# Routing attention and a gated FFN on one core: query halves outermost, exponentials in PSUM, and a weight rounding over three engines

## The chip, the core and the metric

The kernel runs on one core of one Trainium2 chip. A core has a matrix engine (TensorE, PE in the tables, with PEld for its weight loads), a vector engine (VectorE, DVE), a scalar engine (ScalarE, ACT), GpSimd (POOL) and SyncE (SP), which here issues DMAs. SBUF is the working memory, PSUM the memory into which TensorE writes. Each engine runs its own instructions in order, and engines wait for each other by semaphores. The metric is the device time of one execution in microseconds (us); the kernel before takes 1363.32 us, the median of three runs from 1362.93 to 1364.97.

## The reference

Attention over 4 batches and 8 heads, 768 queries and keys, head size 64. Each query and each key is assigned to one of 16 centroids of its head, and a query attends only to keys of its own cluster. The heads' outputs stand side by side as 512 features of 3072 tokens, and an FFN with 2048 hidden units follows.

```
q_assign = argmax(q_n @ c_n.T); k_assign = argmax(k_n @ c_n.T)     # 16 clusters
mask   = q_assign[:, :, :, None] == k_assign[:, :, None, :]
scores = where(mask, (q @ k.T) / sqrt(64), -1e9)
attn   = softmax(scores);  x = attn @ v                            # (4, 8, 768, 64)
h = x.reshape(3072, 512) @ w_in                                    # w_in (512, 2048), float64
out = (h * sigmoid(1.702 * h)) @ w_out                             # w_out (2048, 512), float64
```

The two weights arrive as 64-bit floats and are rounded to 32 bits on the chip from their high and low words.

## The kernel before, in words

Two heads make a pair, 16 pairs in all, four to a batch. A *unit* is 128 keys against half of the queries (384) of a pair: `scores` (L314) gives two 384-column matrix products into a PSUM tile `s`, `weigh` (L325) takes the exponential on ACT into an SBUF tile `A` (L329) and lets DVE zero, in place, what lies outside the cluster, one instruction for each head (L331), `add_up` (L338) adds the units' `A` on POOL for the denominator (L347), and `values` (L350), two units later, multiplies by V (L357). Six units make a *group* (one half of a pair's queries), twelve a pair, 48 a batch, 192 in all. After a group `normalise` (L364) sums over keys on PE (L372), takes the reciprocal on DVE (L375) and scales (L377, L380).

When all eight groups of a batch are there, `ffn_chunks` puts 56 *chunks* into a queue: for each half of the queries 16 of the first product (`first`, L397, with tanh on ACT at L402 and a multiply on DVE at L405) and 12 of the second (`second`, L416: four products of 512 columns each; four such chunks make one block of the output, which is then written out). The loop over units (L444) takes 1.33 chunks a unit from the queue, so that the FFN of a batch runs between the units of the next one. The last batch's 56 chunks run behind everything else (L483).

Preparing a pair (transposes of Q and K, nearest centroid, the codes spread over all partitions as `qb` by a DMA round trip) is eight steps, `PREP`, one a unit, during the pair before (L462). In the same loop, `round_w` (L145) rounds the weights, 64 pieces of 256 columns, 1.5 a unit: DVE masks the bits of the mantissa and shifts the exponent (L153, L155), POOL scales and clamps (L158 to L162), DVE joins (L164 to L168), POOL multiplies (L170).

The order on each engine is the order of the code (the scheduler is set to manual). PSUM has eight banks: two tiles `s` of two banks, one `o`, and three `m` for everything else.

Of the kernel before, what the change touches and what calls it, by code (L numbers as in the profile page):

```python
# [11 lines left out]
U32 = mybir.dt.uint32  # L12
AF = mybir.ActivationFunctionType
# [24 lines left out]
def fast(  # L38
# [58 lines left out]


    qk_in, v_in = {}, {}

    def load_qk(p):
        for w, src in enumerate((q, k)):
            t = inp.tile([P, NJ, 2, D], FP32, name=f"in{w}")
            b, hp = divmod(p, HP)
            for a in range(2):
                nc.sync.dma_start(
                    out=t[:, :, a, :],
                    in_=src[b, 2 * hp + a].rearrange("(p j) d -> p j d", j=NJ))
            qk_in[p, w] = t

    def load_v(p):
        b, hp = divmod(p, HP)
        t = inp.tile([P, 2, NJ, D], FP32, name="inv", bufs=3)
# [6 lines left out]
    cent = const.tile([P, D], FP32, name="cent")  # L120
    nc.scalar.dma_start(out=cent, in_=centroids.rearrange("h c d -> (h c) d"))
    load_qk(0)
    load_v(0)
    load_qk(1)
    load_v(1)

    w_in = const.tile([P, NCH, DF], FP32, name="w_in")
    w_out = const.tile([P, NF, DM], FP32, name="w_out")
    WN = 256
# [6 lines left out]
    w_raw = {}  # L136

    def load_w(i):
        if i < len(w_chunks):
            t = wp.tile([P, WN, 2], I32, name="raw")  # L140
            nc.sync.dma_start(out=t.rearrange("p n t -> p (n t)"),
                              in_=w_chunks[i][1])
            w_raw[i] = t

    def round_w(i):  # L145


        raw = w_raw.pop(i)
        hi, lo = raw[:, :, 1], raw.bitcast(U32)[:, :, 0]
        m, e, one_m = (hp_pool.tile([P, HALF], FP32, name="g")[:, 0:WN]  # L150
                       for _ in range(3))
        m, e = m.bitcast(I32), e.bitcast(I32)
        nc.vector.tensor_scalar(out=m, in0=hi, scalar1=0xFFFFF, scalar2=None,  # L153
                                op0=ALU.bitwise_and)
        nc.vector.tensor_scalar(out=e, in0=hi, scalar1=20, scalar2=0x7FF,  # L155
                                op0=ALU.logical_shift_right,
                                op1=ALU.bitwise_and)
        nc.gpsimd.tensor_scalar(out=one_m, in0=m, scalar1=2.0 ** -20,  # L158
                                scalar2=1.0, op0=ALU.mult, op1=ALU.add)
        nc.gpsimd.tensor_scalar(out=e, in0=e, scalar1=896 + 255.0,  # L160
                                scalar2=896.0, op0=ALU.min, op1=ALU.max)
        nc.gpsimd.tensor_scalar(out=e, in0=e, scalar1=-896.0, scalar2=1.0,  # L162
                                op0=ALU.add, op1=ALU.mult)
        nc.vector.scalar_tensor_tensor(out=one_m, in0=lo, scalar=2.0 ** -52,  # L164
                                       in1=one_m, op0=ALU.mult, op1=ALU.add)
        nc.vector.tensor_scalar(out=e, in0=e, scalar1=23, scalar2=None,  # L166
                                op0=ALU.logical_shift_left)
        nc.vector.scalar_tensor_tensor(out=e, in0=hi, scalar=-2 ** 31, in1=e,  # L168
                                       op0=ALU.bitwise_and, op1=ALU.bitwise_or)
# [3 lines left out]
    for i in range(3):  # L173
        load_w(i)
# [7 lines left out]
    nc.vector.memset(half, 0.5)  # L182
    ones = const.tile([P, D], FP32, name="ones")
# [9 lines left out]
    csq = const.tile([P, D], FP32, name="csq")  # L193
# [9 lines left out]
    cc = const.tile([P, 2, D], FP32, name="cc")  # L203
# [21 lines left out]
    def prep_turn(p, i):  # L225
        w, h = divmod(i, 2)
        if h == 0:
            T[p, w] = trp.tile([P, S], FP32, name=f"T{w}")
# [7 lines left out]
        if h:  # L236
# [4 lines left out]
    def prep_near(p):  # L241
# [11 lines left out]
        sT[p] = asg.tile([P, HALF], FP32, name="sT")  # L253
        nc.scalar.copy(sT[p], ps[:, 0:HALF])

    def prep_assign(p):
# [9 lines left out]
        eq = asg.tile([P, n, NC], FP32, name="eq")  # L266
# [7 lines left out]
        code[p] = asg.tile([P, NH, 2, 2, 2], FP32, name="code")  # L274
# [8 lines left out]
    def prep_spread(p):  # L283
# [6 lines left out]
        row = asg.tile([n, P], BF16, name="row")  # L290
        nc.vector.tensor_copy(out=row, in_=ps[0:n, 0:P])
        line = dram.tile([n, P], BF16, name="line")
        nc.sync.dma_start(out=line, in_=row)
        qb = trp.tile([P, 2, S], BF16, name="qb")
# [7 lines left out]
    PREP += [prep_near, prep_assign, lambda p: None, prep_spread]  # L302


    UP = 2 * NJ
    NU = NPAIR * UP
    s_of, A_of, sum_of, o_of, O_of, xT_of = {}, {}, {}, {}, {}, {}

    def split(u):
        p, r = divmod(u, UP)  # L310
        h, kt = divmod(r, NJ)
        return p, h, kt

    def scores(u):  # L314
        p, h, kt = split(u)
# [7 lines left out]
        s_of[u] = ps[:, :, 0:HALF]  # L323

    def weigh(u):  # L325

        p, h, kt = split(u)
        A = ap.tile([P, 2, HALF], FP32, name="A")
        nc.scalar.activation(out=A, in_=s_of.pop(u), func=AF.Exp, scale=SCALE)  # L329
        for a in range(2):  # L330
# [4 lines left out]
                in1=A[:, a, :], op0=ALU.is_equal, op1=ALU.mult)  # L335
        A_of[u] = A

    def add_up(u):  # L338
        if u % NJ == 0:
            return  # L340
        g = u // NJ
        if u % NJ == 1:
            sum_of[g] = ap.tile([P, 2, HALF], FP32, name="sum", bufs=2)
            first = A_of[u - 1]
        else:
            first = sum_of[g]
        nc.gpsimd.tensor_tensor(out=sum_of[g], in0=first, in1=A_of[u],  # L347
                                op=ALU.add)

    def values(u):  # L350
        p, h, kt = split(u)
        g = u // NJ
# [7 lines left out]
        if kt == NJ - 1:  # L360
            O_of[g] = op.tile([P, HALF], FP32, name="O")
            nc.scalar.copy(O_of[g], o_of.pop(g)[:, 0:HALF])

    def normalise(g):  # L364

        p, h = divmod(g, 2)
        if h == 0:
            xT_of[p] = xp.tile([P, S], FP32, name="xT", bufs=2 * NCH)
# [5 lines left out]
        rec = op.tile([P, HALF], FP32, name="rec")  # L374
        nc.vector.reciprocal(out=rec, in_=ps[:, 0:HALF])  # L375
        O = O_of.pop(g)
        nc.vector.tensor_tensor(out=xT_of[p][:, h * HALF:(h + 1) * HALF],  # L377
                                in0=O, in1=rec, op=ALU.mult)

        nc.vector.scalar_tensor_tensor(  # L380
            out=O, in0=ps[:, 0:HALF], scalar=1.0, in1=rec, op0=ALU.mult,
            op1=ALU.max, accum_out=sums[:, g:g + 1])
        if g % (2 * HP) == 2 * HP - 1:
            ffn.extend(ffn_chunks(p // HP))
# [4 lines left out]
    def ffn_chunks(b):  # L389
        xT = [xT_of.pop(b * HP + c) for c in range(NCH)]  # L390
        hs, ys = {}, {}

        def first(h, f):

            ps = bank()
            for c in range(NCH):
                nc.tensor.matmul(out=ps[:, 0:HALF],  # L397
                                 lhsT=w_in[:, c, f * P:(f + 1) * P],
                                 rhs=xT[c][:, h * HALF:(h + 1) * HALF],
# [37 lines left out]
    for step in PREP:  # L437
        step(0)
# [487 lines left out]
```

## Time and profile before

| what | us |
|---|---|
| median of three runs | 1363.32 |
| the profiled execution | 1362.06 |
| its span, first to last instruction | 1360.3 |
| PE busy | 1170.5 (86%) |
| DVE busy | 618.4 (45%) |
| POOL busy | 446.5 (33%) |
| ACT busy | 271.8 (20%) |
| TensorE's mean granted clock | 0.916 of 2.4 GHz |

The page of the profile gives the busy share of each engine in 40 slices of the span, the granted clock of TensorE beside it, and the groups of instructions by line. A share of the whole span says little here, since the program has stages of different kinds: units with rounding and no FFN, units with FFN, and FFN alone. Each is to be read by itself.

### The profile page before, as it was taken

How to read it: one execution, taken by the hardware profiler on the slowest of the kernel's cores; microseconds unless marked ns; L12 is line 12 of the kernel's file. 1: busy time of each engine (PE TensorE's matmuls, PEld its weight loads, DVE VectorE, ACT ScalarE, POOL GpSimd, SP SyncE). 2: the span in 40 equal slices, each digit the busy share in tenths (PEclk: the TensorE clock that was granted, in tenths of full speed). 3: DMA queues.
4: the chain of work that ended last, by engine and by line, in shares of the span. 5: the costliest groups of instructions: out<-in, count | busy, mean ns of one | idle time of the engine just before them, and what ended most of it. 6: DMA issues, size and time to landing. Idle time of an engine off the chain costs nothing. (4 is left out here: it accounts for less than half of the span.)

```text
span 1360.3 us, 10636 instructions
## 1 busy us (share of the span) xinstructions
PE 1170.5 (86%) x3842; PEld 490.1 (36%) x3842; DVE 618.4 (45%) x1104; ACT 271.8 (20%) x425; POOL 446.5 (33%) x424
## 2 busy tenths in 40 slices
PE   6555455454699999999999999999999999799997
PEld 2111111111244344433443444334434443354553
DVE  4656666667864335434642354356423542320110
ACT  2111111111233113212231132132312321110110
POOL 3666666666632222223322222233222222200000
PEclk8667667677799999999999999999999999899999
DMA  6122222221210010102100101021000000000000
GB/s 163 47 66 82 66 66 70 64 71 59 46 35 13 19 51 1 40 15 62 36 12 20 51 4 44 8 62 35 12 20 16 11 2 16 9 0 14 10 1 25
DMA packets 70095, 49.11 MB, mean 36 GB/s; under 512 B 52624, under 2 KB 56720, under 8 KB 70032
## 3 DMA queue, kind: packets, MB, share of 16 engines
q1 hardware_dynamic: 69888, 48.30, 12.6%
q8 instruction: 32, 0.52, 0.1%
q14 instruction: 31, 0.25, 0.1%
q10 hardware_dynamic: 144, 0.03, 0.0%
HBM read 41.98 MB, written 6.34 MB: 36 GB/s over the span
## 5 line engine op out<-in xcount | busy, mean ns | idle before, releaser
L347 POOL TENSOR_TENSOR sum<-sum,A 128x768 f32<-128x768 f32 x128 | 233.7, 1826 | 437.5 <-DVE A L331 437.5
L331 DVE SCALAR_TENSOR_TENSOR A<-qb,code,A 128x384 f32<-128x384 bf16 x384 | 259.5, 718 | 247.3 <-ACT A L329 242.4
L357 PE MATMUL o<-A,inv 128*64 128x384 f32 x768 | 228.8, 569 | 158.7 <-DVE A L331 139.1
L397 PE MATMUL m<-xT,w_in 128*128 128x384 f32 x1024 | 353.9, 497 | 1.5 <-DVE bad L480 1.1
L416 PE MATMUL m<-w_out,g 128*128 128x512 f32 x768 | 345.3, 600 | 0.0
L329 ACT ACTIVATE A<-s 128x768 f32<-128x768 f32 x192 | 155.6, 810 | 529.7 <-PE s L319 497.6
L397 PEld LDWEIGHTS m<-xT,w_in 128*128 128x128 f32 x1024 | 189.8, 191 | 160.5 <-issue 26.9
L416 PEld LDWEIGHTS m<-w_out,g 128*128 128x128 f32 x768 | 141.6, 190 | 185.4 <-issue 182.6
L319 PE MATMUL s<-T,T 64*128 64x384 f32 x768 | 194.0, 585 | 0.0
L405 DVE SCALAR_TENSOR_TENSOR g<-th,m 128x384 f32<-128x384 f32 x128 | 70.8, 553 | 223.1 <-ACT th L402 222.8
L357 PEld LDWEIGHTS o<-A,inv 128*64 128x64 f32 x768 | 52.8, 147 | 319.5 <-DVE A L331 190.6
L347 POOL TENSOR_TENSOR sum<-A 128x768 f32<-128x768 f32 x32 | 59.5, 1860 | 196.4 <-DVE A L331 194.2
L402 ACT ACTIVATE th<-m 128x384 f32<-128x384 f32 x128 | 62.7, 490 | 264.4 <-PE m L397 260.6
L375 DVE RECIPROCAL rec<-m 128x384 f32<-128x384 f32 x32 | 81.7, 2553 | 34.6 <-PE m L372 34.6
L319 PEld LDWEIGHTS s<-T,T 64*128 64x128 f32 x768 | 63.8, 204 | 87.0 <-issue 72.3
L164 DVE SCALAR_TENSOR_TENSOR g<-raw,g 128x256 f32<-128x256 uint32 x64 | 27.2, 425 | 62.8 <-POOL g L158 62.8
L160 POOL TENSOR_SCALAR g<-g 128x256 int32<-128x256 int32 x64 | 40.8, 638 | 5.1
L166 DVE TENSOR_SCALAR g<-g 128x256 int32<-128x256 int32 x64 | 18.8, 294 | 49.8 <-POOL g L162 49.8
L422 ACT ACTIVATE y<-m 128x512 f32<-128x512 f32 x24 | 14.3, 597 | 128.6 <-PE m L416 115.5
L231 PE MATMUL m<-ident,in 128*128 128x128 f32 x192 | 39.4, 323 | 0.3 <-DMA in<-in_k_dram 0.2
L170 POOL TENSOR_TENSOR w_out<-g 128x256 f32<-128x256 f32 x32 | 29.9, 933 | 27.9 <-DVE g L168 27.9
L170 POOL TENSOR_TENSOR w_in<-g 128x256 f32<-128x256 f32 x32 | 29.5, 923 | 27.9 <-DVE g L168 27.9
(54 smaller groups left out, 381.7 us busy)
## 6 DMA issues: line engine op xcount, KB each, us to landing
raw<-in_moe_w_in_dram SPq DMA_DIRECT2D x32, 256.0 KB, 2.7
raw<-in_moe_w_out_dram SPq DMA_DIRECT2D x32, 256.0 KB, 2.6
in<-in_q_dram SPq DMA_DIRECT2D x32, 192.0 KB, 4.1
in<-in_k_dram SPq DMA_DIRECT2D x32, 192.0 KB, 4.3
inv<-in_v_dram SPq DMA_DIRECT2D x16, 384.0 KB, 3.2
qb<-line SPq DMA_DIRECT2D x16, 384.0 KB, 3.5
out_dram<-y SPq DMA_DIRECT2D x24, 256.0 KB, 2.0
line<-row SPq DMA_DIRECT2D x16, 3.0 KB
```

What stands on the lines that cost most here:

```text
L160: nc.gpsimd.tensor_scalar(out=e, in0=e, scalar1=896 + 255.0, scalar2=896.0, op0=ALU.min, op1=ALU.max)
L170: nc.gpsimd.tensor_tensor(out=w_chunks[i][0], in0=one_m, in1=e.bitcast(FP32), op=ALU.mult)
L319: nc.tensor.matmul(out=ps[:, a, 0:HALF], lhsT=T[p, 1][rows, kt * P:(kt + 1) * P], rhs=T[p, 0][rows, h * HALF:(h + 1) * HALF], start=True, ...
L329: nc.scalar.activation(out=A, in_=s_of.pop(u), func=AF.Exp, scale=SCALE)
L331: nc.vector.scalar_tensor_tensor(out=A[:, a, :], in0=qcode[p][:, a, h * HALF:(h + 1) * HALF], scalar=code[p][:, kt % NH, 1, kt // NH, a:a ...
L347: nc.gpsimd.tensor_tensor(out=sum_of[g], in0=first, in1=A_of[u], op=ALU.add)
L357: nc.tensor.matmul(out=o_of[g][a * D:(a + 1) * D, 0:HALF], lhsT=v_in[p][:, a, kt, :], rhs=A[:, a, :], start=(kt == 0), stop=(kt == NJ - 1))
L375: nc.vector.reciprocal(out=rec, in_=ps[:, 0:HALF])
L397: nc.tensor.matmul(out=ps[:, 0:HALF], lhsT=w_in[:, c, f * P:(f + 1) * P], rhs=xT[c][:, h * HALF:(h + 1) * HALF], start=(c == 0), stop=(c = ...
L402: nc.scalar.activation(out=th, in_=ps[:, 0:HALF], func=AF.Tanh, scale=0.851)
L405: nc.vector.scalar_tensor_tensor(out=g, in0=th, scalar=1.0, in1=ps[:, 0:HALF], op0=ALU.add, op1=ALU.mult)
L416: nc.tensor.matmul(out=ps[:, 0:DM], lhsT=hs[h, f][:, n * P:(n + 1) * P], rhs=w_out[:, f, :], start=(f == 0), stop=(f == NF - 1))
```

## The change

A pair's two query halves are no longer done one behind the other. Within a batch all four pairs are done for the first half, then all four for the second, and after four groups the FFN of that half (28 chunks) enters the queue. The loop turns once for two units (*turn t*, 96 in all, three to a group, 12 to a half): two units' scores and exponentials, half of the turn's FFN chunks, preparation steps, rounding, two units' masks and sums, two units' values of the turn before, a normalisation where one is due, and the other FFN chunks. The chunk rate is 28 in 11.5 turns.

The exponential is written back over the scores in PSUM, and the mask reads it there and writes `A` in SBUF. The codes `qb` are 8-bit. The weights are rounded in 32 pieces of 512 columns: DVE cuts the exponent and the mantissa out (`split_w`), ACT scales both, DVE joins the piece before (`join_w`), and POOL does the one multiply. Two thirds of a piece a turn are rounded in the first 12 turns, 2.3 a turn after that. Two pairs are prepared ahead of the loop, pairs 2 and 3 in turns 0 to 5, later ones 20 to 1 turns or so ahead at one step a turn.

```diff
-    def round_w(i):
-        raw = w_raw.pop(i)
...
-        nc.gpsimd.tensor_tensor(out=w_chunks[i][0], in0=one_m,
-                                in1=e.bitcast(FP32), op=ALU.mult)
+    def split_w(i):
+        hi = w_raw[i][:, :, 1]
+        w = w_chunks[i][0]
+        e = wp.tile([P, WN], I32, name="e", bufs=2)
+        nc.vector.tensor_scalar(out=e, in0=hi, scalar1=EXP, scalar2=None,
+                                op0=ALU.bitwise_and)
+        nc.vector.tensor_scalar(out=w.bitcast(I32), in0=hi, scalar1=0xFFFFF,
+                                scalar2=None, op0=ALU.bitwise_and)
+        nc.scalar.activation(out=e, in_=e, func=AF.Relu, scale=8.0,
+                             bias=low[:, 0:1])
+        nc.scalar.activation(out=w, in_=w.bitcast(I32), func=AF.Copy,
+                             scale=2.0 ** -20, bias=1.0)
+    def join_w(i):
+        raw, e, w = w_raw.pop(i), w_pow.pop(i), w_chunks[i][0]
+        nc.vector.scalar_tensor_tensor(
+            out=e, in0=raw[:, :, 1], scalar=-2 ** 31, in1=e,
+            op0=ALU.bitwise_and, op1=ALU.bitwise_or)
+        nc.vector.scalar_tensor_tensor(
+            out=w, in0=raw.bitcast(U32)[:, :, 0], scalar=2.0 ** -52, in1=w,
+            op0=ALU.mult, op1=ALU.add)
+        nc.gpsimd.tensor_tensor(out=w, in0=w, in1=e.bitcast(FP32),
+                                op=ALU.mult)
+    def round_to(n):
+        while w_done[0] <= min(n, NW):
+            i = w_done[0]
+            if i < NW:
+                load_w(i + 2)
+                split_w(i)
+            if i:
+                join_w(i - 1)
+            w_done[0] += 1
...
+        s = s_of[u] = ps[:, :, 0:HALF]
+        nc.scalar.activation(out=s, in_=s, func=AF.Exp, scale=SCALE)
...
-        nc.scalar.activation(out=A, in_=s_of.pop(u), func=AF.Exp, scale=SCALE)
...
-                in1=A[:, a, :], op0=ALU.is_equal, op1=ALU.mult)
+                in1=s[:, a, :], op0=ALU.is_equal, op1=ALU.mult)
...
-    for u in range(NU + DEN):
...
+    for t in range(NT + 2):
+        us = range(2 * t, 2 * t + 2) if t < NT else ()
+        for u in us:
+            scores(u)
+        owed = owed + rate if ffn else 0.0
+        n = min(int(owed), len(ffn))
+        owed -= n
+        for _ in range((n + 1) // 2):
+            ffn.popleft()()
+        for p, i in prep_at.get(t, ()):
+            prep(p, i)
+        round_to(int(t * 2 / 3 if t < TB / 2 else
+                     TB / 3 + (t - TB / 2) * 2.3) - 1)
+        for u in us:
+            mask(u)
+        if 1 <= t <= NT:
+            for u in range(2 * t - 2, 2 * t):
+                values(u)
+        if t >= 2 and (t - 2) % TG == TG - 1:
+            normalise((t - 2) // TG)
+        for _ in range(n // 2):
+            ffn.popleft()()
```

On PE, where the first FFN chunks stand (`s` scores, `o` values, `m<-x,w_in` or `m<-xT,w_in` an FFN chunk of four products), the kernel before has one unit at a time:

```order
L319 MATMUL s<-T_1547,T_1624 128x384 x2
L397 MATMUL m<-xT,w_in 128x384 x4
L357 MATMUL o<-A,inv 64x384 x2
L259 MATMUL m<-ident,sT 128x128 x3
L319 MATMUL s<-T_1547,T_1624 128x384 x2
L397 MATMUL m<-xT,w_in 128x384 x4
L357 MATMUL o<-A,inv 64x384 x2
L319 MATMUL s<-T_1547,T_1624 128x384 x2
L397 MATMUL m<-xT,w_in 128x384 x8
L357 MATMUL o<-A,inv 64x384 x2
```

On PE in the changed kernel, turns 14 to 16, the first with FFN:

```order
L344 MATMUL s<-T_151,T_165 128x384 x4
L417 MATMUL m<-x,w_in 128x384 x4
L379 MATMUL o<-A,inv 64x384 x4
L417 MATMUL m<-x,w_in 128x384 x4
L344 MATMUL s<-T_209,T_223 128x384 x4
L417 MATMUL m<-x,w_in 128x384 x4
L379 MATMUL o<-A,inv 64x384 x4
L417 MATMUL m<-x,w_in 128x384 x4
L344 MATMUL s<-T_209,T_223 128x384 x4
L417 MATMUL m<-x,w_in 128x384 x8
```

The scores of two units now stand together, and so do the values of two units; FFN chunks stand between them on both sides. The two score tiles of a turn are both of the two that exist.

On DVE, the rounding ahead of a unit's masks (L331) in the stage without FFN, in the kernel before, with two pieces:

```order
L153 TENSOR_SCALAR g<-raw 128x256
L155 TENSOR_SCALAR g<-raw 128x256
L164 SCALAR_TENSOR_TENSOR g<-raw,g 128x256
L166 TENSOR_SCALAR g<-g 128x256
L168 SCALAR_TENSOR_TENSOR g<-raw,g 128x256
L153 TENSOR_SCALAR g<-raw 128x256
L155 TENSOR_SCALAR g<-raw 128x256
L164 SCALAR_TENSOR_TENSOR g<-raw,g 128x256
L166 TENSOR_SCALAR g<-g 128x256
L168 SCALAR_TENSOR_TENSOR g<-raw,g 128x256
L331 SCALAR_TENSOR_TENSOR A<-qb,code,A 128x384 x2
```

On DVE in the changed kernel, turn 15: the FFN multiplies (L424, one of turn 14 and one of turn 15), two pieces split and joined, and the masks of two units (L358, four instructions):

```order
L424 SCALAR_TENSOR_TENSOR g<-g,m 128x384 x2
L158 TENSOR_SCALAR e<-raw 128x512
L160 TENSOR_SCALAR w_in<-raw 128x512
L170 SCALAR_TENSOR_TENSOR e<-raw,e 128x512
L173 SCALAR_TENSOR_TENSOR w_in<-raw,w_in 128x512
L158 TENSOR_SCALAR e<-raw 128x512
L160 TENSOR_SCALAR w_in<-raw 128x512
L170 SCALAR_TENSOR_TENSOR e<-raw,e 128x512
L173 SCALAR_TENSOR_TENSOR w_in<-raw,w_in 128x512
L358 SCALAR_TENSOR_TENSOR A<-qb,code,s 128x384 x4
```

A piece's joining (L170, L173) now stands behind the splitting of the next piece, so it reads what ACT made earlier. The masks of the turn stand behind all of it, and behind the multiply of the turn's first FFN chunk.

## Rows read from the trace of the kernel before

**Rows 1.** the stages by windows: engines' busy us (instructions), granted clock, DMA share, GB/s

```profile
13.60:374.90 361.30, 194.64 (x554) 59.80 (x553) 240.44 (x486) 52.56 (x74) 230.96 (x298) 0.70 0.23 67
374.90:1173.60 798.70, 798.24 (x2802) 339.49 (x2800) 349.08 (x558) 195.96 (x307) 211.62 (x118) 1.00 0.09 25
1173.60:1184.60 11.00, 4.19 (x20) 1.21 (x18) 5.61 (x10) 1.29 (x2) 2.61 (x2) 0.78 0.06 22
1184.60:1352.50 167.90, 167.84 (x448) 86.37 (x448) 17.73 (x32) 18.66 (x37) 0.00 (x0) 0.98 0.02 9
```

**Rows 2.** timeline, stage without FFN: start, length, engine, line, [idle before <-releaser]

```profile
184.98 0.43 DVE L164 SCALAR_TENSOR_TENSOR g<-raw,g 128x256 f32<-128x256 uint32 x1 [0.37 <-POOL g L158]
...
186.19 0.29 DVE L166 TENSOR_SCALAR g<-g 128x256 int32<-128x256 int32 x1 [0.78 <-POOL g L162]
...
187.52 2.54 PE L357 MATMUL o<-A,inv 128*64 128x384 f32 x4 [7.41 <-DVE A L331]
```

**Rows 3.** timeline of PE where FFN sets in, same columns

```profile
363.95 2.07 PE L357 MATMUL o<-A,inv 128*64 128x384 f32 x4 [1.89 <-DVE A L331]
...
366.79 1.18 PE L319 MATMUL s<-T,T 64*128 64x384 f32 x4
...
374.05 0.92 PE L319 MATMUL s<-T,T 64*128 64x384 f32 x4
374.90 2.85 PE L397 MATMUL m<-xT,w_in 128*128 128x384 f32 x8
377.67 0.87 PE L357 MATMUL o<-A,inv 128*64 128x384 f32 x4
...
389.76 5.43 PE L397 MATMUL m<-xT,w_in 128*128 128x384 f32 x16
```

**Rows 4.** timeline of the start: first work, masks, rounding, POOL beside them

```profile
5.00 1.51 PE L231 MATMUL m<-ident,in 128*128 128x128 f32 x6
...
13.66 1.65 PE L319 MATMUL s<-T,T 64*128 64x384 f32 x4
...
18.87 1.15 DVE L331 SCALAR_TENSOR_TENSOR A<-qb,code,A 128x384 f32<-128x384 bf16 x2 [4.88 <-DMA qb<-line]
...
26.17 0.72 POOL L170 TENSOR_TENSOR w_in<-g 128x256 f32<-128x256 f32 x1 [0.87 <-DVE g L168]
26.21 0.84 DVE L155 TENSOR_SCALAR g<-raw 128x256 int32<-128x256 int32 x1
...
29.29 1.61 DVE L331 SCALAR_TENSOR_TENSOR A<-qb,code,A 128x384 f32<-128x384 bf16 x2
...
31.05 1.80 POOL L347 TENSOR_TENSOR sum<-sum,A 128x768 f32<-128x768 f32 x1 [0.56 <-DVE A L331]
31.29 1.71 DVE L153 TENSOR_SCALAR g<-raw 128x256 int32<-128x256 int32 x1
```

**Rows 5.** groups by line: busy, mean ns | idle before, releaser

```profile
L375 DVE RECIPROCAL rec<-m 128x384 f32<-128x384 f32 x32 | 81.7, 2553 | 34.6 <-PE m L372 34.6
L405 DVE SCALAR_TENSOR_TENSOR g<-th,m 128x384 f32<-128x384 f32 x128 | 70.8, 553 | 223.1 <-ACT th L402 222.8
...
L402 ACT ACTIVATE th<-m 128x384 f32<-128x384 f32 x128 | 62.7, 490 | 264.4 <-PE m L397 260.6 <-DVE A L331 3.8
...
L164 DVE SCALAR_TENSOR_TENSOR g<-raw,g 128x256 f32<-128x256 uint32 x64 | 27.2, 425 | 62.8 <-POOL g L158 62.8
...
L166 DVE TENSOR_SCALAR g<-g 128x256 int32<-128x256 int32 x64 | 18.8, 294 | 49.8 <-POOL g L162 49.8
...
L471 DVE TENSOR_SCALAR ok<-sums 128x32 f32<-128x32 f32 x1 | 0.2, 180 | 0.0
```

**Rows 6.** the same, from 374.9 to 1173.6

```profile
L397 PE MATMUL m<-xT,w_in 128*128 128x384 f32 x768 | 268.3, 496 | 0.5 <-DVE O L380 0.3
L416 PE MATMUL m<-w_out,g 128*128 128x512 f32 x576 | 262.6, 602 | 0.0
```

**Rows 7.** timeline of PE at the end of the attention

```profile
1173.62 1.51 PE L357 MATMUL o<-A,inv 128*64 128x384 f32 x8
```

More of the change, by code (lines that the diff above doesn't have):

```diff
@@ L12 @@
 U32 = mybir.dt.uint32
+U8 = mybir.dt.uint8
 AF = mybir.ActivationFunctionType
@@ L227, in prep_turn @@
         if h == 0:
-            T[p, w] = trp.tile([P, S], FP32, name=f"T{w}")
+            T[p, w] = pairs.tile([P, S], FP32, name=f"T{w}")
         ps = bank()
@@ L424, in second @@
                     out=out[b * S:(b + 1) * S, :].rearrange(
-                        "(p j) n -> p j n", j=NJ)[:, j, :], in_=y)
-        chunks = []
-        for h in range(2):
-            chunks += [lambda h=h, f=f: first(h, f) for f in range(NF)]
-            chunks += [lambda j=j, part=part: second(j, part)
-                       for j in range(h * NH, (h + 1) * NH)
-                       for part in range(NF // 4)]
-        return chunks
-    for step in PREP:
-        step(0)
-    LAG = 2
@@ L440, in fast @@
-    DEN = 4
-    rate = (2 * NF + NJ * (NF // 4)) / (HP * UP - 6)
-    owed = 0.0
-    w_next = 0
-    for u in range(NU + DEN):
-        p, r = divmod(u, UP)
-        if u < NU:
-            scores(u)
-            if r == 0 and p + 2 < NPAIR:
-                load_qk(p + 2)
-            if r == 3 and p + 2 < NPAIR:
-                load_v(p + 2)
-            weigh(u)
-            add_up(u)
+                        "(p j) n -> p j n", j=NJ)[:, h * NH + n, :], in_=y)
+        return ([lambda f=f: first(f) for f in range(NF)]
+                + [lambda n=n, part=part: second(n, part)
+                   for n in range(NH) for part in range(NF // 4)])
@@ new lines, in fast @@
+    NT = NU // 2
+    TG = NJ // 2
+    TB = 2 * HP * TG
+    prep_at = {}
+    for p in range(2, NPAIR):
+        b, hp = divmod(p, HP)
+        for i, step in enumerate(PREP):
+            if b == 0:
+                t = (hp - 2) * TG + i * TG // len(PREP)
+            else:
+                t = b * TB + (-20, -8, -2, 1)[hp] + i
+            prep_at.setdefault(t, []).append((p, i))
+    loads = deque((p, w) for p in range(NPAIR) for w in range(2))
+    for _ in range(3):
+        loads.popleft()
@@ L454, in fast, with prep @@
+    def prep(p, i):
+        if i == 0 and p:
+            load_v(p)
+        PREP[i](p)
+        if i in (1, 3) and loads:
+            load_qk(*loads.popleft())
+    rate = (NF + NH * (NF // 4)) / (TB / 2 - 0.5)
+    owed = 0.0
+    for p in range(2):
+        for i in range(len(PREP)):
+            prep(p, i)
+    for t in range(NT + 2):
+        us = range(2 * t, 2 * t + 2) if t < NT else ()
+        for u in us:
+            scores(u)
         owed = owed + rate if ffn else 0.0
-        while owed >= 1.0 and ffn:
+        n = min(int(owed), len(ffn))
+        owed -= n
+        for _ in range((n + 1) // 2):
```

201 lines of the change are left out of this document (87 added, 114 removed).

## The prediction

> **What bounds the kernel now.** I read the profile in stages, first by windows, since the page's slices show two kinds of stretch: PE half busy at a granted clock near 0.7, then PE full at 1.00. The rows by stage [rows 1] are to be seen as five prices. From 13.6 to 374.9 us 52 units run without any FFN, 6.95 us each; PE is busy 195 of 361 us, at a clock that switches between the two levels of 1.2 and 2.4 GHz, DVE 240 and POOL 231. From 374.9 to 1173.6 the other 140 units run with 168 FFN chunks, PE is busy all the time at 2.4 GHz, and DVE 349 of 799 us. Then come 11 us for the last group and the check, 167.9 us of FFN alone (56 chunks, 3.0 us each), and from 1352.5 the last write, 7.8 us to the span's end.
>
> The timeline of the first stage says why it is slow [rows 2]: within one rounding piece DVE waits for POOL (0.37 us ahead of L164, 0.78 ahead of L166), since the two pass it back and forth, the masks of the unit stand behind it on DVE, and PE's values wait 7.41 us for the masks. Where rounding has ended and FFN has not set in [rows 3], three units take 374.05 - 366.79 = 7.26 us, 2.42 each, with a preparation and a normalisation among them. So the first stage is bound by DVE and POOL taking turns at the weights, the second by PE, and the fourth by PE.
>
> **The change, part by part.** The sum is over the same five stages, from the start on.
>
> *Start.* Two pairs are prepared ahead of the first unit, where there was one. The first pair takes from 5.00 to 13.66 us [rows 4]; the second repeats these 8.7 us on the same chain of engines. First unit: 22 us (18 if half of it fits into the waits of the first, 28 if K of pair 1, now behind two 512 KB weight loads on SP's queue, comes late).
>
> *Units without FFN.* These are now the 14 turns before a half batch is normalised, 28 units instead of 52. Per turn: two units at 2.42 us, 4.84; ahead of its masks two thirds of a rounding piece. Price of a piece of 512 columns: the plain mask instruction is 180 ns at 32 columns and 294 at 256 [rows 5], so about 0.42 us at 512; the two-tensor one 425 ns at 256 and 553 at 384, so about 0.69. Two of each make 2.2 us, and the ping-pong with POOL goes, since a piece is joined a step after ACT has scaled it. POOL keeps one multiply: 0.72 us at 256 columns, 1.80 for a sum of 768 [rows 4], so about 1.26. Two thirds of 2.2, with some blocking by POOL, is 1.8 us a turn. The codes of pairs 2 and 3 are spread in the turn in which they are found, so PE waits twice for DVE; I put 0.4 a turn for it. 4.84 + 1.8 + 0.4 = 7.0, times 14 = 98 us. Ends: 68 (the rounding hides beside PE) and 126 (9 a turn, PE at 1.2 GHz: scores 1.65 and values 2.54 us [rows 4, 2], twice, and a little).
>
> *Units with FFN.* 164 units (28 to 191) and seven halves, 196 chunks: 112 of the first product and 84 of the second. Prices from this stage alone [rows 6]: 268.3 / 96 = 2.79 us for a first chunk, 262.6 / 72 = 3.65 for a second one, and what is left of 798.7, 267.8 / 140 = 1.91, for a unit with its share of preparation and normalising. 313 + 306 + 314 = 933 us. Two units' values in a row take 1.51 us where one takes 0.87 [rows 7, 3], 0.23 saved in a turn; if scores in a row do the same, 82 turns save 38, if neither carries over, none. I take the middle, 19: 914 us.
>
> *What is late next.* Score tiles are now held until the masks have read them, and there are two, both used in a turn. So a turn is at least: two scores, the FFN chunks of its first part, tanh, multiply, rounding, the first unit's masks; then PE may write scores again. Without rounding that is 1.7 + 2.79 + 0.49 + 0.55 [rows 5] + 1.1 = 6.6 us, beside 9.4 of PE work in a turn with two chunks, and 9.2 beside 12.2 with three (two adjacent first chunks are 5.43 [rows 3]): hidden, with 3 us to spare. If that cover went, each microsecond over would cost 82.
>
> In turns 14 to 22 the cover does go, since 24 of the 32 pieces are rounded there. Within a burst a piece costs more: a plain mask beside a POOL multiply took 0.84 us [rows 4], where a like one alone takes 0.29 [rows 2], 0.55 more behind a 0.72 us multiply, so about 1.1 more behind one of 1.26. First piece of a turn 2.2, each later one 3.3: two 5.5, three 8.8. Turns 14, 15 and 17 (two chunks, two pieces): chain 1.7 + 2.8 + 1.0 + 5.5 + 1.1 = 12.2 against 9.4, 2.8 of waiting each. Turns 18 and 20 (three chunks, two pieces): 14.8 against 12.2 and 13.0, 2.6 and 1.8. Turns 16 and 19 (three pieces): about 6 each. In turns 21 and 22 the second product itself waits for its last weights, seven pieces in two turns: 5 and 7. Sum 37. After a wait PE runs slow for a while: behind one of 1.89 us the values took 2.07 instead of 0.87 and the scores 1.18 instead of 0.92 [rows 3]; some 1 us for each of nine turns, 9. Together 46, with ends 0 (FFN chunks and values fill it) and 85.
>
> *Masks and exponentials.* A pair of masks took 1.15 us with POOL idle and 1.61 beside a POOL multiply [rows 4]; with one tensor in PSUM, as L405 has it at 553 ns [rows 5], I count 0.57 each. In the stage with FFN this is worth nothing, as DVE has over half of its time free there; without FFN it is inside the 7.0. The exponential's place costs nothing on ACT, the idlest engine of the four. Eight-bit codes halve a transfer that is early anyway.
>
> This is also where a rule bears on the sum. Beside a POOL sum of 1.80 us that started first, a plain mask of DVE took 1.71 us instead of 0.29 [rows 4, 2], which is all of the sum's remainder, while the two-tensor masks were only slowed. The Trainium skill (SBUF — State Buffer, Who interferes with whom) says that DVE and GpSimd share one pair of ports, that a DVE instruction in a two-port mode or with two SBUF inputs contends with GpSimd, and that the second to issue blocks fully until the first is done. The plain mask agrees (1.71 beside 1.80); the two-tensor one at 1.61 for two is milder than that. By the rule taken fully the masks' move into PSUM frees them, and the split instructions are the losers; what that would cost is a rival below.
>
> *End.* The last group and the check stay, 11 us. Behind them 28 chunks are left instead of 56: 167.9 / 2 = 84. Last write 8; outside the span 2 (1362.06 - 1360.3).
>
> **Sum.** 22 + 98 + 914 + 46 + 11 + 84 + 8 + 2 = 1185 us, against 1362.06 of the profiled execution; that lies 1.3 us below the median of 1363.3, so the forecast can be held against either.
>
> **The rivals.**
> - *No waits in turns 14 to 22.* DVE has 24 pieces at 2.2, masks, multiplies and normalisings, about 94 us of work (53, 20, 9 and 11) beside some 108 of PE's there; if chunks and values always stand ready, the 46 go, and scores in a row save the other 19: 1120. For it: values of the turn before and the turn's later chunks do not depend on the masks. Against it: PE's order is fixed, and the next scores stand in front of them.
> - *POOL blocks the splits fully.* Each of the 24 pieces meets a sum as well as a multiply, 1.42 more each (1.71 - 0.29), all on the turn's chain: 34, so 1219. For it the 1.71 row; against it that sums follow the masks at once and are mostly done when the next turn's rounding begins.
> - *The held score tiles bind every turn.* Slower than before: exponential, multiply of the first chunk, masks and a normalisation (2.55 us for the reciprocal alone [rows 5]) in one line on DVE, so that PE waits before each turn's scores and falls to 1.2 GHz behind it. It decides from (1363 - 1185) / 73 = 2.4 us in each of the other 73 turns; 2 us of waiting and 1 of slow clock are 219, 1404. Against it the 3 us to spare.
> - *The change does not bring its order about*: a pool or a queue ties the second half's FFN to the first batch's end, so that stages stay as long as they were, 1363.
>
> **How the numbers follow.** Forecast 0.66, no waits 0.14, full blocking 0.13, held tiles 0.05, no change 0.02. Predicted 1185, its own range 1150 to 1225 from the ends of start, head and waits. The 8-in-10 range takes in the first two rivals and part of the head's ends: 1130 to 1245. A measurement here cannot tell 0.2% from no change; faster by more 0.93, within it 0.02, slower 0.05.
>
> **What would show it.** The first FFN chunk near 120 us; 28 units before it at about 7 us a turn; PE full from about turn 23 on, with 11 to 12 us a turn; in the nine turns before, PE waiting for the masks (L358) or, at the end of them, for rounded weights; masks near 0.57 us each; the FFN alone at the end 84 us. It is wrong if PE waits before scores in later turns, if the stage without FFN is far from 98, or if the nine turns take 115 us or over 190.

## The result, and the profile after

The changed kernel takes 1185.88 us, the median of four runs from 1183.65 to 1186.97. The kernel before took 1363.49 beside it, so the ratio is 0.8694, with a 95% interval from 0.8679 to 0.8709: 178 us less. The forecast was 1185. The profiled execution took 1185.81 us with a span of 1184.0, and PE is busy 1090.9 us of it (92%) at a mean granted clock of 0.959.

The windows of the changed kernel stand in the same columns as those of before [rows 1]: length, then the busy us (instructions) of PE, PEld, DVE, ACT and POOL, the granted clock, the DMA share and GB/s. The stages are the units without FFN, the turns in which rounding and FFN meet, the turns with FFN alone, the end of the attention, and the FFN behind it.

```profile
23.46:126.39 102.93, 73.04 (x313) 29.48 (x312) 75.80 (x129) 41.55 (x65) 53.57 (x32) 0.80 0.36 96
126.39:281.00 154.61, 113.42 (x349) 50.03 (x349) 88.93 (x165) 51.00 (x85) 58.86 (x39) 0.84 0.27 79
281.00:1087.00 806.00, 803.85 (x2901) 364.69 (x2899) 327.05 (x555) 198.73 (x326) 220.67 (x122) 1.00 0.08 22
1087.00:1093.70 6.70, 4.66 (x13) 1.61 (x14) 4.47 (x8) 0.60 (x1) 0.00 (x0) 1.00 0.10 39
1093.70:1178.00 84.30, 84.28 (x224) 43.26 (x224) 8.88 (x16) 9.05 (x18) 0.00 (x0) 0.98 0.02 7
```

The stage without FFN went from 361 us to 103, and the FFN alone from 168 to 84. Between them PE is full at 2.4 GHz for 806 us. In the first stretch PE idles 30 us; the stretch with FFN work at hand that is still loose is the second, in which it idles 41 of 155 us. The timeline of PE there, turn by turn (start, length, engine, line and operation, tiles, shape, and in brackets the idle time before and what ended it), where the kernel before had waits of 7.41 us ahead of its values [rows 2]:

```profile
123.53 2.93 PE L344 MATMUL s<-T,T 64*128 64x384 f32 x8 [4.82 <-DVE A L358]
126.39 3.46 PE L417 MATMUL m<-x,w_in 128*128 128x384 f32 x8
...
137.39 2.70 PE L344 MATMUL s<-T,T 64*128 64x384 f32 x8 [3.32 <-DVE A L358]
...
151.03 2.70 PE L344 MATMUL s<-T,T 64*128 64x384 f32 x8 [3.31 <-DVE A L358]
...
171.06 2.93 PE L344 MATMUL s<-T,T 64*128 64x384 f32 x8 [6.15 <-DVE A L358]
...
218.52 2.93 PE L344 MATMUL s<-T,T 64*128 64x384 f32 x8 [5.61 <-DVE A L358]
...
235.26 2.18 PE L344 MATMUL s<-T,T 64*128 64x384 f32 x8 [1.70 <-DVE A L358]
...
248.68 1.13 PE L434 MATMUL m<-w_out,g 128*128 128x512 f32 x2 [3.35 <-POOL w_out L176]
...
280.29 1.56 PE L344 MATMUL s<-T,T 64*128 64x384 f32 x8
281.78 7.13 PE L434 MATMUL m<-w_out,g 128*128 128x512 f32 x16
...
1086.89 0.87 PE L391 MATMUL m<-sum,ones 128*64 128x384 f32 x4
1087.68 3.70 PE L434 MATMUL m<-w_out,g 128*128 128x512 f32 x8
1092.21 0.27 PE L511 MATMUL m<-ident,ok 128*1 128x128 f32 x1 [0.82 <-ACT y L440]
1093.72 3.50 PE L417 MATMUL m<-x,w_in 128*128 128x384 f32 x5 [1.25 <-DVE bad L515]
```

The first FFN chunk comes at 126.39 us. The scores of each following turn wait for the masks of the turn before, and the second product at the end of the rounding waits for its weights. At 280.29 the scores follow without a wait, in 1.56 us instead of 2.70. What DVE does ahead of the masks of turn 14 is to be seen in the timeline of DVE and POOL:

```profile
130.41 0.56 DVE L424 SCALAR_TENSOR_TENSOR g<-g,m 128x384 f32<-128x384 f32 x1 [2.06 <-ACT g L422]
130.88 0.42 DVE L158 TENSOR_SCALAR e<-raw 128x512 int32<-128x512 int32 x1
131.22 0.42 DVE L160 TENSOR_SCALAR w_in<-raw 128x512 int32<-128x512 int32 x1
...
131.55 0.69 DVE L170 SCALAR_TENSOR_TENSOR e<-raw,e 128x512 int32<-128x512 int32 x1
...
132.16 0.69 DVE L173 SCALAR_TENSOR_TENSOR w_in<-raw,w_in 128x512 f32<-128x512 uint32 x1
132.92 1.27 POOL L176 TENSOR_TENSOR w_in<-w_in,e 128x512 f32<-128x512 f32 x1 [5.59 <-DVE w_in L173]
134.22 0.43 DVE L158 TENSOR_SCALAR e<-raw 128x512 int32<-128x512 int32 x1 [1.38 <-POOL w_in L176]
...
136.11 2.18 DVE L358 SCALAR_TENSOR_TENSOR A<-qb,code,s 128x384 f32<-128x384 uint8 x4
```

A piece is 2.2 us of DVE, as forecast, and the second of a burst begins 1.38 us late. It waits for POOL's multiply to end, since the tile `e` that the split writes has two buffers and the multiply still reads one of them. The groups by line (mean ns behind the busy us, then idle time before and its releasers) give the masks at 607 ns and the wait of the split, 22.4 us in all:

```profile
L358 DVE SCALAR_TENSOR_TENSOR A<-qb,code,s 128x384 f32<-128x384 uint8 x384 | 209.7, 607 | 132.7 <-ACT s L349 101.7 <-issue 30.9
L158 DVE TENSOR_SCALAR e<-raw 128x512 int32<-128x512 int32 x32 | 15.8, 495 | 22.4 <-POOL w_out L176 13.9 <-POOL w_in L176 8.5
```

### The profile page after: what moved, and what is told of

Read it like the earlier page. It is cut to its first block, busy times and chain, and to the rows that moved or that the text cites. A ratio compares the mean times of both kernels' runs of the same rounds, so it can differ in the third digit from the quotient of the medians.

```text
span 1184.0 us, 10396 instructions
## 1 busy us (share of the span) xinstructions
PE 1090.9 (92%) x3842; PEld 495.7 (42%) x3842; DVE 513.4 (43%) x897; ACT 306.6 (26%) x505; POOL 334.5 (28%) x200
## 5 line engine op out<-in xcount | busy, mean ns | idle before, releaser
L434 PE MATMUL m<-w_out,g 128*128 128x512 f32 x768 | 355.3, 610 | 14.9 <-POOL w_out L176 14.9
L417 PE MATMUL m<-x,w_in 128*128 128x384 f32 x1024 | 362.7, 503 | 1.4 <-DVE bad L515 1.2
L358 DVE SCALAR_TENSOR_TENSOR A<-qb,code,s 128x384 f32<-128x384 uint8 x384 | 209.7, 607 | 132.7 <-ACT s L349 101.7
L417 PEld LDWEIGHTS m<-x,w_in 128*128 128x128 f32 x1024 | 190.4, 194 | 172.7 <-issue 42.1
L344 PE MATMUL s<-T,T 64*128 64x384 f32 x768 | 169.3, 554 | 49.5 <-DVE A L358 47.4
L349 ACT ACTIVATE s<-s 128x768 f32<-128x768 f32 x192 | 145.9, 794 | 239.8 <-PE s L344 239.8
L424 DVE SCALAR_TENSOR_TENSOR g<-g,m 128x384 f32<-128x384 f32 x128 | 70.8, 553 | 276.9 <-ACT g L422 276.9
L379 PE MATMUL o<-A,inv 128*64 128x384 f32 x768 | 150.6, 515 | 0.0
L422 ACT ACTIVATE g<-m 128x384 f32<-128x384 f32 x128 | 62.8, 491 | 307.7 <-PE m L417 307.7
L394 DVE RECIPROCAL short<-m 128x384 f32<-128x384 f32 x32 | 81.6, 2550 | 34.0 <-PE m L391 34.0
L176 POOL TENSOR_TENSOR w_out<-w_out,e 128x512 f32<-128x512 f32 x16 | 20.6, 1289 | 58.2 <-DVE w_out L173 58.2
L162 ACT ACTIVATE e<-e,low 128x512 int32<-128x512 int32 x32 | 23.1, 721 | 49.1 <-DVE e L158 48.9
L176 POOL TENSOR_TENSOR w_in<-w_in,e 128x512 f32<-128x512 f32 x16 | 20.3, 1267 | 53.8 <-DVE w_in L173 53.8
```

The source lines that it names most:

```text
L176: nc.gpsimd.tensor_tensor(out=w, in0=w, in1=e.bitcast(FP32), op=ALU.mult)
L344: nc.tensor.matmul(out=ps[:, a, 0:HALF], lhsT=T[p, 1][rows, kt * P:(kt + 1) * P], rhs=T[p, 0][rows, h * HALF:(h + 1) * HALF], start=True, ...
L349: nc.scalar.activation(out=s, in_=s, func=AF.Exp, scale=SCALE)
L358: nc.vector.scalar_tensor_tensor(out=A[:, a, :], in0=qcode[p][:, a, h * HALF:(h + 1) * HALF], scalar=code[p][:, kt % NH, 1, kt // NH, a:a ...
L379: nc.tensor.matmul(out=o_of[g][a * D:(a + 1) * D, 0:HALF], lhsT=v_in[p][:, a, kt, :], rhs=A[:, a, :], start=(kt == 0), stop=(kt == NJ - 1))
L417: nc.tensor.matmul(out=ps[:, 0:HALF], lhsT=w_in[:, c, f * P:(f + 1) * P], rhs=xT[c], start=(c == 0), stop=(c == NCH - 1))
```

## The experiments

Eight kernels were run, five in four timed executions each and three in two. Each is one edit of the changed kernel, except the fourth, which edits the kernel before.

**1. Rounding behind the masks.** In a turn the call of `round_to` goes behind the masks.

```diff
-        round_to(int(t * 2 / 3 if t < TB / 2 else
-                     TB / 3 + (t - TB / 2) * 2.3) - 1)
         for u in us:
             mask(u)
+        round_to(int(t * 2 / 3 if t < TB / 2 else
+                     TB / 3 + (t - TB / 2) * 2.3) - 1)
```

> The rounding of a turn is put behind the turn's masks, nothing else is changed. Theory A (the waits of PE before the scores in turns 14 to 22 come from the rounding standing ahead of the masks on DVE): the waits for the masks in turns 13 to 20, 3 to 6 us each and some 35 us with turn 13's, nearly vanish, the waits of the second product for its last weights stay (about 15 us), and the whole falls by 25 to 45 us, to 1140 to 1160. Rival B (DVE simply has too much work in these turns, wherever the rounding stands): the wait moves to another place, such as banks held by the FFN multiplies, and the time stays within 10 us of 1186.

Measured: 1182.36 us (1177.35 to 1183.75), ratio 0.867, interval 0.8646 to 0.8694. The idle time ahead of the scores that ends with a mask falls from 47.4 us to 13.0, and yet the median is only 3.5 us lower, which is not clear of the spread of the runs. That is the rival's case, within 10 us of 1186. The waits moved, above all to what stands behind the rounding on DVE, the scaling and the reciprocal's follow-up of a normalisation: PE now idles 17.8 us ahead of the chunks of the first product, 13.2 ahead of transposes and 6.0 ahead of values, where the changed kernel has 1.4, 2.0 and 0.0 (timeline of PE in this kernel):

```profile
133.81 1.65 PE L417 MATMUL m<-x,w_in 128*128 128x384 f32 x2 [5.94 <-DVE x L396]
...
178.55 0.87 PE L254 MATMUL m<-ident,in 128*128 128x128 f32 x3 [9.80 <-DVE short L398]
```

And the rounding itself became dearer, since POOL adds up the masked units while DVE splits (timeline of DVE and POOL in this kernel):

```profile
150.88 0.42 DVE L158 TENSOR_SCALAR e<-raw 128x512 int32<-128x512 int32 x1
151.11 1.86 POOL L368 TENSOR_TENSOR sum<-A 128x768 f32<-128x768 f32 x1 [3.39 <-PE s L344]
151.22 2.03 DVE L160 TENSOR_SCALAR w_in<-raw 128x512 int32<-128x512 int32 x1
```

The split that starts before the sum takes 0.42 us, its twin that starts 0.11 us after it takes 2.03 and ends 0.28 us behind the sum. So where the rounding stands decides what it pays: ahead of the masks it holds the scores, behind them it runs into the sums.

**2. Exponentials back in SBUF.** ACT writes `A` in SBUF, and the masks work in place there.

```diff
-        s = s_of[u] = ps[:, :, 0:HALF]
-        nc.scalar.activation(out=s, in_=s, func=AF.Exp, scale=SCALE)
+        A = s_of[u] = ap.tile([P, 2, HALF], FP32, name="A")
+        nc.scalar.activation(out=A, in_=ps[:, :, 0:HALF], func=AF.Exp,
+                             scale=SCALE)
```

> The exponential goes into A in SBUF as in the kernel before, and the masks work on A in place; the rest is the changed kernel. Theory A: score tiles come free after the exponential, so PE's waits before scores go, and what waits instead is the values of the next turn, later by scores and one FFN chunk (4.5 us): the nine turns lose 20 to 35 us of waiting, the masks get slower beside POOL (0.65 to 0.8 us instead of 0.55), which costs some 5 us in the stage without FFN; 1155 to 1175. Rival B (leaving the exponentials in PSUM is what makes the masks cheap and the kernel fast): 1195 or more.

Measured: 1180.64 us (1178.93 to 1181.97), ratio 0.8662, interval 0.8648 to 0.8677. Neither expectation held. The masks are 104 us dearer on DVE and the kernel is 5 us faster (groups by line of this kernel):

```profile
L358 DVE SCALAR_TENSOR_TENSOR A<-qb,code,A 128x384 f32<-128x384 uint8 x384 | 313.6, 877 | 113.4 <-ACT A L349 113.4
L344 PE MATMUL s<-T,T 64*128 64x384 f32 x768 | 154.4, 522 | 0.0
```

Scores now wait for nothing, 0.0 us against 49.5, as a score tile is free when ACT has read it. What was won there is mostly lost on the late DVE: an FFN chunk waits 9.44 us for a normalisation's product at 133.80, another 10.15 at 218.33. From the scores of turn 23 to the last chunk ahead of the end it takes 812.7 us (273.27 to 1085.99) where the changed kernel takes 811.1, so there DVE has the room for dearer masks. The 14 turns without FFN are 2.3 us shorter, the nine turns behind them 4.2. The edit makes the masks dearer and frees the score tiles earlier, both at once, so that only the net of the two is shown: the place of the exponential, which made each mask 270 ns cheaper, bought no time here.

**3. No rounding.** The two weights are set to a constant once and their raw words are still loaded; split, join and multiply are left out.

```diff
+    nc.gpsimd.memset(w_in, 0.01)
+    nc.gpsimd.memset(w_out, 0.01)
...
                 load_w(i + 2)
-                split_w(i)
-            if i:
-                join_w(i - 1)
+                w_raw.pop(i)
```

> The weights are loaded but not rounded: two memsets set both weights to a constant instead, so the output is not the reference's. Theory A: all of the rounding's cost goes: the 41 us of waits in turns 14 to 22, some 10 to 15 us of slow clock behind them, and about 1.8 us a turn of 14 without FFN: 1186 - 41 - 12 - 25 = 1108 (1095 to 1125). Rival B (the stage without FFN is bound by scores, exponential and masks in a chain, not by rounding): that stage stays near 7 us a turn and only the 41 to 55 go: 1130 to 1145.

Measured: 1108.99 us, ratio 0.8138, interval 0.8122 to 0.8154, as the first theory had it. The windows of this kernel (columns as above) are the 14 turns without FFN and what follows to 281 us:

```profile
34.00:109.90 75.90, 60.55 (x305) 24.18 (x304) 50.61 (x90) 28.84 (x44) 38.58 (x22) 0.91 0.50 138
109.90:281.00 171.10, 170.44 (x646) 80.09 (x646) 76.42 (x128) 46.34 (x78) 48.15 (x27) 1.00 0.27 88
```

Without rounding the 14 turns take 75.9 us, 5.4 each, against 100.1 (7.15 each), and PE is full from the first chunk on. The turns 14 to 22, from scores to scores, take 93.48 us at a granted clock of 1.00, against 156.76 in the changed kernel (123.53 to 280.29); the timeline of PE in this kernel:

```profile
109.91 1.56 PE L344 MATMUL s<-T,T 64*128 64x384 f32 x8
...
203.39 1.56 PE L344 MATMUL s<-T,T 64*128 64x384 f32 x8
```

The setting of the weights delays the first scores to 34.0 us, some 11 us that the kernel with rounding doesn't pay. So rounding costs the changed kernel 77 us by the totals, and 88 with that delay set aside; all waits of the turns 14 to 22 are its doing.

**4. The old order with the new rounding.** The kernel before, with `split_w` and `join_w` in pieces of 512 columns, three quarters of a piece a unit (cut to its core).

```diff
-        while w_next < min(len(w_chunks), (3 * u + 1) // 2):
-            load_w(w_next + 3)
-            round_w(w_next)
+        while w_next < min(NW + 1, (3 * u + 1) // 4):
+            if w_next < NW:
+                load_w(w_next + 2)
+                split_w(w_next)
+            if w_next:
+                join_w(w_next - 1)
```

> The kernel before with the changed kernel's rounding (32 pieces, three quarters of a piece a unit; the tanh goes into the same tile as the multiply to make room), in the old order of units. Theory A (the order alone is worth about half): the first stage falls from 6.95 to about 4.2 us a unit with rounding and 2.4 without, 361 to some 205 to 230 us, the rest stays: 1205 to 1235. Rival B (the gain is almost all the order's, the FFN-less stage of 52 units is the loss): 1290 or more. Rival C (the rounding alone does it all): 1190 or less.

Measured: 1249.15 us, ratio 0.9167, interval 0.9148 to 0.9185. This lies between the expectations, 14 us above the nearest. Two like instructions of one shape give one reason why it was dearer than the sum (groups by line of this kernel):

```profile
L155 DVE TENSOR_SCALAR w_out<-raw 128x512 int32<-128x512 int32 x16 | 18.0, 1122 | 0.0
L153 DVE TENSOR_SCALAR e<-raw 128x512 int32<-128x512 int32 x32 | 13.3, 415 | 0.0
```

In this order the second split often starts just after a POOL sum has, and takes 2.03 us there, as in experiment 1. Some 0.7 us more in each of 32 pieces is an estimate of 23 us of DVE; how much of that shows in the kernel's time was not measured. The lighter rounding alone gives 114 of the 178 us.

**5. A third buffer for `e`.** The 1.38 us ahead of a split are either a wait for a buffer, or the port that DVE and POOL share, as the prediction had it.

```diff
-        e = wp.tile([P, WN], I32, name="e", bufs=2)
+        e = wp.tile([P, WN], I32, name="e", bufs=3)
```

> The exponent's tile e gets a third buffer, nothing else. In the changed kernel the splits of a burst's later pieces wait for POOL's multiply of the piece before (22.4 us in all, some 1.4 each). Theory A (a semaphore wait through the two buffers of e, with the shared port just behind it): that wait vanishes, but the second of the two plain masks then runs beside the multiply and is blocked until it ends, about 1 us instead of 0.42, so little is gained: 1178 to 1187. Rival B (the port has no part in it): each later piece costs 2.2 again, 13 x 1.4 go: 1165 to 1172.

Measured: 1180.58 us (1178.85 to 1181.69), ratio 0.8655, interval 0.8641 to 0.867, inside the first theory's 1178 to 1187. The timeline of DVE and POOL in this kernel, at the second piece of turn 14:

```profile
131.25 0.42 DVE L158 TENSOR_SCALAR e<-raw 128x512 int32<-128x512 int32 x1
131.42 1.38 POOL L176 TENSOR_TENSOR w_in<-w_in,e 128x512 f32<-128x512 f32 x1 [5.71 <-DVE w_in L173]
131.59 1.50 DVE L160 TENSOR_SCALAR w_in<-raw 128x512 int32<-128x512 int32 x1
```

The split's wait for POOL is gone (2.9 us in the whole run, from 22.4), and at once the other cause shows: the second split starts behind the multiply and takes 1.50 us instead of 0.42, 1.08 more. Both are there; the wait stood first and covered the port. That is why so little is won: over the run DVE's idle time ahead of the first splits falls by 16.9 us (22.4 to 5.5), and all the splits together get 10.6 us dearer (32.4 to 43.0). The Trainium skill (SBUF — State Buffer, Who interferes with whom) says that of DVE in a two-port mode and GpSimd the second to issue blocks fully until the first is done; the plain splits agree here and in experiment 1, and one in experiment 8 does not.

**6. The multiply on DVE.** This takes POOL out of the rounding altogether, wait and port alike.

```diff
-        nc.gpsimd.tensor_tensor(out=w, in0=w, in1=e.bitcast(FP32),
+        nc.vector.tensor_tensor(out=w, in0=w, in1=e.bitcast(FP32),
                                 op=ALU.mult)
```

> The last multiply of a piece runs on DVE instead of POOL. Theory A (DVE's own time binds turns 14 to 22, POOL's multiply costs only through the splits that wait for it): 0.69 more for each piece, 1.4 less for each later piece of a burst, and 0.6 less of waiting for the last weights in turns 21 and 22: 1178 to 1190. Rival B (POOL is what stretches these turns): 1160 to 1172.

Measured: 1186.51 us (1185.03 to 1189.96), ratio 0.8709, interval 0.8694 to 0.8723: no difference, inside the first theory's 1178 to 1190. The groups by line of this kernel:

```profile
L158 DVE TENSOR_SCALAR e<-raw 128x512 int32<-128x512 int32 x32 | 15.6, 487 | 1.3 <-DMA raw<-in_moe_w_out_dram 0.9
L176 DVE TENSOR_TENSOR w_in<-w_in,e 128x512 f32<-128x512 f32 x16 | 11.1, 692 | 0.6
```

No wait for POOL is left, and 0.69 us a piece stands on DVE instead, on the same chain ahead of the masks. Two pieces take 5.3 us (133.66 to 138.99 in the timeline) where they took 5.2 (130.88 to 136.11).

**7. The new order with the old rounding.** The changed kernel with the `round_w` of before, in 64 pieces of 256 columns (cut to its core).

```diff
     def round_to(n):
-        while w_done[0] <= min(n, NW):
-            i = w_done[0]
...
+        while w_done[0] < min(2 * n, NW):
+            load_w(w_done[0] + 3)
+            round_w(w_done[0])
             w_done[0] += 1
```

> The changed kernel with the rounding of the kernel before (64 pieces of 256 columns, DVE and POOL in turns), two old pieces at the places of one new one; the pieces of the second weight go row block by row block. Theory A (order and rounding add up): old pieces cost some 3.3 us each in DVE's order, so 6.6 for two against 2.2 to 3.6: about 10 x 4 in the first 14 turns and 22 x 3 in the next nine, 1290 (1265 to 1315), so that order and rounding alone are worth about 70 and 114. Rival B (the new order hides the rounding beside FFN, whatever its form): 1230 or less.

Measured: 1303.99 us, ratio 0.9562, interval 0.9543 to 0.9581, as expected. With experiment 4 this makes a square:

| us | old order | new order |
|---|---|---|
| old rounding | 1363 | 1304 |
| new rounding | 1249 | 1186 |

Rounding gives 114 or 118 us, the order with all else 59 or 63. The two add up: neither needs the other.

**8. Masks, then rounding, then sums.** The turn masks first, rounds with three buffers for `e`, and only then issues POOL's sums, which were part of `mask` so far.

```diff
-        e = wp.tile([P, WN], I32, name="e", bufs=2)
+        e = wp.tile([P, WN], I32, name="e", bufs=3)
...
         A_of[u] = A
+
+    def add_up(u):
...
+        for u in us:
+            mask(u)
         round_to(int(t * 2 / 3 if t < TB / 2 else
...
         for u in us:
-            mask(u)
+            add_up(u)
```

> Masks first, then the rounding (with the third e buffer), then POOL's sums of the turn, so that the sums stand behind the multiplies on POOL. With the rounding behind the masks alone, the first plain masks of a turn stood beside POOL's sums, 1.26 and 2.03 us instead of 0.42 each. Theory A (DVE's time is what binds, and this blocking is what ate that version's gain): 2.4 us a turn come back over 11 turns, 1150 to 1165. Rival B (the wait only moves on, to the sums that the normalisation needs): 1175 or more.

Measured: 1158.27 us (1156.52 to 1159.79), ratio 0.8497, interval 0.8483 to 0.8511. It beats both kernels, by 205 and by 28 us, inside the first theory's 1150 to 1165. The timeline of DVE and POOL in this kernel, one burst:

```profile
145.67 2.18 DVE L358 SCALAR_TENSOR_TENSOR A<-qb,code,s 128x384 f32<-128x384 uint8 x4
147.77 0.42 DVE L158 TENSOR_SCALAR e<-raw 128x512 int32<-128x512 int32 x1
148.10 0.42 DVE L160 TENSOR_SCALAR w_in<-raw 128x512 int32<-128x512 int32 x1
...
149.64 0.43 DVE L158 TENSOR_SCALAR e<-raw 128x512 int32<-128x512 int32 x1
149.82 4.14 POOL L176 TENSOR_TENSOR w_in<-w_in,e 128x512 f32<-128x512 f32 x2 [5.60 <-DVE w_in L173]
149.98 0.43 DVE L160 TENSOR_SCALAR w_in<-raw 128x512 int32<-128x512 int32 x1
...
150.31 0.70 DVE L170 SCALAR_TENSOR_TENSOR e<-raw,e 128x512 int32<-128x512 int32 x1
```

In this burst the splits take 0.42 or 0.43 us each, neither piece waits, and they follow each other in 1.9 us. Over the run all the splits take 39.0 us of DVE, against 62.9 in experiment 1 and 32.4 in the changed kernel, and no wait for POOL is left ahead of them, where those two have 20.7 and 22.4 us; the scores' idle time is 11.7 us against the changed kernel's 49.5. The multiply is the one that is slowed in the burst shown (1823 and 1586 ns in the run's means by line, against 1289 and 1267), on an engine that has the time. One split, at 149.98, starts 0.16 us behind a multiply and still takes 0.43, where its like in experiment 5, 0.17 us behind one, took 1.50: here the multiply was held instead. At 114.69 us of this same kernel a split 0.19 us behind a multiply took 1.49. Which of the two is held in such a meeting, these runs don't settle. Of the three parts of this edit, the move alone gave 3.5 us (experiment 1, not clear of noise) and the buffer alone 5 (experiment 5); the sums' new place was not run alone. What is left above experiment 3 are slower first turns (90.5 us from the first scores, at 22.80, to the first FFN chunk, against 77.4 there) and waits for normalisations and for the second product's weights, as this timeline of PE shows:

```profile
160.04 0.87 PE L254 MATMUL m<-ident,in 128*128 128x128 f32 x3 [6.41 <-DVE short L402]
...
223.84 3.78 PE L438 MATMUL m<-w_out,g 128*128 128x512 f32 x4 [7.41 <-POOL w_out L176]
```

## Why the prediction was right, step by step

The total came out to a microsecond, the sign and the mechanism of the gain as forecast, and none of the rivals came true. But the hit is in good part luck: terms that were too small by about 21 us in all, 13 of them slow clock, stand against terms too large by about 20.

| step | forecast, us | measured, us | read from |
|---|---|---|---|
| start, to the first scores | 22 | 23.5 | timeline of PE |
| 14 turns without FFN | 98 | 100.1 | 23.46 to 123.53 |
| units with FFN at full clock | 914 | 904.6 | 93.48 of experiment 3, and 280.29 to 1091.38 |
| waits in turns 14 to 22 | 37 | 40.9 | timeline of PE |
| slow clock behind them | 9 | 22.4 | the rest of 123.53 to 280.29 |
| end of the attention | 11 | 2.3 | 1091.38 to 1093.72 |
| FFN alone | 84 | 84.3 | 1093.70 to 1178.00 |
| last write, and outside the span | 10 | 7.8 | 1178.0 to 1185.81 |

- **The head.** 7.15 us a turn against 7.0. It is made up as forecast: 5.4 without rounding (experiment 3; the forecast had 5.2 with its 0.4 for the codes) and 1.7 for two thirds of a piece with what it adds in slow clock, 0.80 granted here and 0.91 there (forecast 1.8).
- **The waits.** The scores of turns 15 to 21 waited 3.32, 3.31, 6.15, 2.99, 2.98, 5.61 and 1.70 us, the forecast for the turns ahead of them was 2.8, 2.8, 6, 2.8, 2.6, 6 and 1.8: 26.1 in all against 24.8. The second product's weights cost 14.9 (9.0 and 5.9), forecast 12. So 41 against 37. The slow clock behind a wait was taken too small: in turn 15 scores took 2.70 us instead of 1.56 and the first chunk 3.47 instead of 2.85, 1.8 together where 1 stood. Over all nine turns it is 22.4 us against 9: 156.76 us, less the 93.48 that the same products take in experiment 3 without a wait, less 40.9 of waits. This term of the sum was off most.
- **Why a piece in a burst costs more.** Right in size (1.1 forecast, 1.38 measured) and wrong in cause. The prediction put it down to the port. What the changed kernel paid was a wait for one of `e`'s two buffers, and the port's 1.08 us stepped in only when experiment 5 took that wait away. The row from which the prediction drew its 0.55 us [rows 4] showed a real effect, at another place than the one where it was spent. The semaphore could have been read from the code, where two buffers serve three steps, split, join and multiply.
- **Units with FFN.** Forecast 914, at full clock 904.6: 93.5 for turns 14 to 22 (experiment 3) and 811.1 from there to the last chunk. Scores in a row start their successor after 1.49 us (280.29 to 281.78), two single ones would need 1.70 (twice 374.05 to 374.90 [rows 3]), so their saving carried over beside that of the values, and 28 of the possible 38 us came, where the middle value had 19.
- **The end.** This step failed: 11 us forecast, 2.3 measured. The prediction kept the 11 us of before, in which the last group's normalisation ran with nothing beside it. In the new order the chunks of the half before are still in the queue: behind L391 at 1086.89 another chunk of the second product follows at 1087.68, and covers the reciprocal. The turn's own order, in which the other half of its chunks stands behind the normalisation, would have said so.
- **The masks in PSUM.** Forecast 0.57 us each and worth nothing in the stage with FFN. They took 0.545 in a row of four (2.18) and 607 ns in the mean, and experiment 2, where the masks cost DVE 104 us more and the score tiles come free earlier, is no slower.
- **The rivals.** *No waits* fell by the waits above; of the kernels run only experiment 3, which leaves the rounding out, came below its time, with 1109. The 108 us of PE work that this rival counted in these turns were 93.5 in experiment 3, and its pieces are 22 and not 24, since ten are split before turn 14 (L158 in the trace: 10 before 123.53, 22 from there to 280.29). *Full blocking* fell because the sums were mostly over when the splits began (means of 495 and, for the second split, 620 and 421 ns); experiments 1 and 4 show the same splits at 2.03 us where a sum comes first, so the rival's price was about right (1.61 us more at this width, against 1.42) and its condition not met. *Held tiles in every turn* fell by the third window: PE busy 803.85 of 806 us.

## What to carry to other kernels

Price a changed order by stage, and ask at each engine's fixed order what stands behind the slow work and who waits for it: moving the rounding behind the masks only moved the wait, and it paid when the sums were moved and a buffer was added as well. Before a stall beside another engine is put down to contention, count the buffers of the tile between them; one more buffer is the experiment that tells, and it may only uncover the contention beneath. An engine's time that a change saves (104 us on DVE here) is worth what the engine's waiters gain, and holding the source longer can take it back.

## What the runs showed of the hardware

- The same plain DVE split of 512 columns took 0.42 us alone, 1.50 behind a POOL multiply of 1.38 us and 2.03 behind a POOL sum of 1.86: in both it ends 0.3 us behind POOL's instruction. One that had started 0.23 us ahead of the sum was not touched. In experiment 8 two splits that started 0.16 and 0.19 us behind a multiply took 0.43 and 1.49.
- A mask with both tensors in SBUF took 877 ns in the mean, with one of them in PSUM 607. An exponential from PSUM to PSUM took 794 ns, to SBUF 808.
- Behind a wait of 3.32 us the scores and the chunk that followed ran partly at 1.2 GHz: the windows show a mean of 0.60, then 0.81, and then 1.00, the 2.4 GHz at which PE had run before the wait:

```profile
137.39:140.02 2.63, 2.63 (x8) 0.60 0.50 179
140.02:143.42 3.40, 3.40 (x10) 0.81 0.00 0
143.42:147.64 4.22, 4.22 (x17) 1.00 0.08 11
```

The columns are length, PE's busy us (instructions), granted clock, DMA share and GB/s, in the changed kernel. Here 3.3 us of waiting cost 1.8 more behind it. Over the turns 14 to 22 it is 22.4 us behind 40.9, so that the waits cost about half as much again as their own length.
